# A gated recurrence and a maxout layer on one core: a shorter weight conversion, joined output sums, column quarters, and new instruction lists

## The chip, the cores and the metric

The kernel runs on one core of a Trainium2 chip. A core has five engines with queues of their own: TensorE (PE in the profile; its weight loads appear as PEld), VectorE (DVE), ScalarE (ACT), GpSimd (POOL) and SyncE (SP, which here only issues DMAs). Each engine takes its instructions in program order, and they wait for each other by semaphores. The metric is device time in microseconds (us); the profile is one execution, recorded by the hardware profiler.

## The reference

The first half is a recurrence over 768 time steps for 4 batches of 8 heads, with states of 48 x 48:

```python
mag = np.sqrt(a_re * a_re + a_im * a_im)
scale = np.minimum(mag, 0.999) / (mag + 1e-06)
a_re_n, a_im_n = (a_re * scale, a_im * scale)
for t in range(S):
    new_re = ar * S_re - ai * S_im
    new_im = ar * S_im + ai * S_re
    kv = np.einsum('bhd,bhe->bhde', k[:, :, t], v[:, :, t])
    S_re, S_im = (new_re + kv, new_im)
    y[:, :, t] = np.einsum('bhd,bhde->bhe', q[:, :, t], S_re)
```

The second half takes the 3072 rows of 384 features that come out and computes

```python
h = np.maximum(np.maximum(x @ w1, x @ w2), x @ w3)
return (h @ w_out).astype(np.float32)
```

with 768 hidden features. The weights arrive as float64; everything else is float32.

## The kernel before

The sequence is cut into 24 chunks of 128 steps. Two chunks (x and y, from two batches) make a group; there are 12 groups, six along the sequence for each pair of batches. A step is named by a word, such as `csx:3`: step `cs`, chunk x, group 3.

The steps of a group, with the engine that does them:

- Gates (`gates`): `sqr sqi add lnL expw expe lne relu Lnop abs addw lnw expL mulai mulw stt atan turn` and a few more make the logarithm of the gate's size (tile `Ln`) and its angle in turns (tile `w`) from `a_re` and `a_im`. ACT does the functions, DVE the products, and two of the sums are DMAs from POOL that add in memory.
- Angles (`angles`): `cs` sums the turns along the chunk on PE, by a product with a triangular matrix: four products for a chunk, each with 64 output columns of the array and 192 moving elements. `t`, `nf`, `af`, `sa`, `sb` take off whole turns and make cosine and sine.
- Decays (`turns`): `sums` and `F` on PE sum `Ln` over parts of the chunk; `En Ek Eq` and `f0` to `f3` are their exponentials on ACT. `mk mq uk uq kEn` scale k and q by them on DVE; `tpk tpq` transpose on PE, `Kc Qc` copy the result out of PSUM.
- Scores (`factors`, `scores`): `Q1 Q2 KB QB QG` on DVE, `A` and `B` on PE, `g0` to `g3` (DVE) and `b0 b1` (ACT) fill the masked score tile `atm`.
- State and output (`state`, `outputs`): `dk` on PE, `h0` to `h3` on DVE carry the state in tiles `g`; `y` on PE gives the chunk's output, transposed, and `x` copies it into `xhx`, the features.
- Maxout layer (`up`, `seven`): `U11 U12 U01 U02` are each nine products of 256 tokens (the first digit is the half of the hidden features, the second the weight matrix); `u..` takes the larger of the two on ACT (relu) or DVE. x @ w1 is subtracted from the other two matrices beforehand (`Wg`), and its own way to the output (w1 @ w_out) is multiplied out once (`T`, `t`, `M`, `m`), so that only two matrices are left in the loop. The projection to the output is Strassen's scheme in Winograd's form: sums `S1` to `S4` on DVE, products `P1` to `P7` (four matmuls each) and `Px Py` on PE, and output sums `r1 r6 r5 r7 r57 ox oy`; `D` stores. Group 0 is done without it (`up_one`, `project`), while the sums of weights (`J`) are made.
- Weights (`weight_load`, `weight_step`): twelve blocks of 128 x 768 numbers are loaded as float64 (`WL0` to `WL11`) and turned into float32 by integer work on their two words. Step `a` (ACT) takes the size of the high word, scaled; `b` (DVE) limits it; `c` (DVE) shifts it by three bits; `e` (DVE) fills in bits of the low word; `f` (DVE) puts the sign back and writes the block to its place.

All of this is one list of words, `SCHEDULE`, that the program runs through from front to back. The class `Bound` ties each instruction to the one ahead of it on the same engine, so the list is the order of every engine's queue, the DMA queues of SP and POOL among them. `SLOTS` names, for each PSUM tile in the order in which they are made, which of four places (two banks each) it gets; `OTHER` holds the words that run on the second engine that can do them (copies, relu and absolute values on DVE, loads and sums elsewhere).

Two things in the code matter for reading the profile. Products of few rows or columns use a part of the array, by the partitions where operands and output lie, and several run at a time. The profile gives this form with every matmul, as 128*64 for 128 rows and 64 columns. And float32 products are recorded as two matmuls each.

Every operation is recorded with the line of the helper class, L210, so groups are told apart by tile names: `up` (U), `op` (P, Px, Py, O), `ot` (the output rows), `strassen` (S1 to S4), `xhx` (features, hidden features, and in the start the tile on which the weights are converted).

Of the kernel before, what the change touches and what calls it, by code (L numbers as in the profile page):

```python
# [13 lines left out]
I32 = mybir.dt.int32  # L14
# [7 lines left out]
Lrx:0 Lix:0 sqi0:0 WL0:0 sqr0:0 xor0:0 add0:0 Wa0:0 Wb0:0 Wc0:0 We0:0 Liy:0 Wf0:0 lnL0:0 expw0:0 expe0:0 relu0:0  # L22
lne0:0 Lnop0:0 Zf:0 Lry:0 sqi1:0 xor1:0 sqr1:0 WL3:0 abs0:0 add1:0 Wa3:0 half0:0 Wb3:0 Wc3:0 lnL1:0 expe1:0 expw1:0
We3:0 lne1:0 relu1:0 Lnop1:0 Wf3:0 pw0:0 lnw0:0 expL0:0 mulai0:0 abs1:0 Lrx:1 half1:0 WL6:0 mulw0:0 Liy:1 Wa6:0
Wb6:0 sumsx:0 stt0:0 Eqx:0 Wc6:0 pw1:0 lnw1:0 expL1:0 Ekx:0 mulw1:0 WL9:0 Wa9:0 mulai1:0 We6:0 Fx:0 f1x:0 sumsy:0
Wb9:0 Eny:0 Enx:0 stt1:0 T1:0 Wf6:0 Wc9:0 f0x:0 atan0:0 turn0:0 Lqx:0 csx:0 mqx:0 WL10:0 Wa10:0 We9:0 Wf9:0 atan1:0
turn1:0 Lry:1 sqr:1 t1:0 WL11:0 Lkx:0 tx:0 nfx:0 Wa11:0 Wb10:0 csy:0 afx:0 sax:0 mkx:0 Wb11:0 Wc10:0 Lix:1 sbx:0
uqx:0 sqi:1 Lix:2 Wc11:0 Lky:0 tpqx:0 ty:0 add:1 f3x:0 f2x:0 ukx:0 Fy:0 Qcx:0 We10:0 Wf10:0 nfy:0 tpkx:0 We11:0
lnL:1 WL2:0 Q2x:0 kEnx:0 Eqy:0 expe:1 Eky:0 relu:1 xor:1 expw:1 QBx:0 Kcx:0 abs:1 T2:0 T0:0 t0:0 CL:0 KBx:0 WL1:0
Wa1:0 pw:1 Q1x:0 mky:0 Wb1:0 f0y:0 f1y:0 Wc1:0 t2:0 f2y:0 Wf11:0 lne:1 Lnop:1 Ax:0 g0x:0 Lry:2 g1x:0 We1:0 g2x:0  # L30
half:1 Lqy:0 Cdx:0 f3y:0 Liy:2 Lvx:0 mqy:0 Wa2:0 Wb2:0 lnw:1 expL:1 M0:0 mulw:1 Wc2:0 M1:0 mulai:1 dkx:0 Wf1:0
stt:1 afy:0 say:0 sby:0 Wg1:0 sqi:2 WL4:0 Wa4:0 g3x:0 sumsx:1 Lrx:2 Cdy:0 sqr:2 M2:0 We2:0 QGx:0 atan:1 Wb4:0 Wf2:0
Lvy:0 Eqx:1 Enx:1 Ekx:1 uky:0 Zg:0 tpky:0 h1x:0 m0:0 m1:0 Lkx:2 Z3:0 Wg2:0 Wc4:0 uqy:0 tpqy:0 Lqx:1 Kcy:0 Qcy:0
Bx:0 b0x:0 turn:1 b1x:0 h2x:0 mqx:1 Fx:1 f0x:1 We4:0 f1x:1 Wf4:0 f2x:1 add:2 csx:1 tx:1 yx:0 KBy:0 Q2y:0 nfx:1 xx:0
h3x:0 f3x:1 lnL:2 expe:2 Q1y:0 WL5:0 Wa5:0 Lkx:1 sumsy:1 csy:1 Eky:1 ty:1 Ay:0 kEny:0 Wb5:0 WL7:0 relu:2 mkx:1
g0y:0 Wc5:0 expw:2 U01x:0 nfy:1 abs:2 u01x:0 Lvy:1 We5:0 Eqy:1 Z2:0 g1y:0 Wa7:0 QBy:0 afy:1 Wf5:0 Eny:1 g2y:0 g3y:0
Wb7:0 Wg4:0 U11x:0 xor:2 By:0 dky:0 U02x:0 Lvx:1 b1y:0 h1y:0 b0y:0 QGy:0 yy:0 addw:2 lnw:2 expL:2 xy:0 U11y:0 Wg5:0
u02x:0 U02y:0 afx:1 half:2 u11x:0 Wc7:0 lne:2 We7:0 mulw:2 mulai:2 sbx:1 h2y:0 Z4:0 sax:1 h3y:0 stt:2 atan:2 Wf7:0
U12x:0 u12x:0 say:1 sby:1 Cdy:1 WL8:0 Cdx:1 turn:2 ukx:1 uqx:1 U01y:0 u01y:0 u11y:0 Wa8:0 U12y:0 csy:2 ty:2 u12y:0
csx:2 tpqx:1 tx:2 u02y:0 Qcx:1 nfy:2 Lnop:2 nfx:2 tpkx:1 Fy:1 kEnx:1 Wb8:0 Wc8:0 We8:0 Kcx:1 Wg7:0 Wf8:0 U21y:0  # L40
Wg8:0 KBx:1 f0y:1 u21y:0 Lky:1 Lqy:1 mky:1 afy:2 sumsx:2 dkx:1 Q1x:1 f1y:1 f2y:1 f3y:1 Enx:2 U21x:0 u21x:0 afx:2
U22y:0 u22y:0 Oy:0 Lqx:2 mqy:1 uky:1 uqy:1 tpqy:1 Ekx:2 Lix:3 Q2x:1 say:2 sby:2 sbx:2 sax:2 Eqx:2 h0x:1 h1x:1 QGx:1
h2x:1 oy:0 QBx:1 mkx:2 h3x:1 Qcy:1 Q1y:1 tpky:1 Kcy:1 Ax:1 g0x:1 Q2y:1 Liy:3 sqi:3 Fx:2 sumsy:2 g1x:1 g2x:1 U22x:0
Lrx:3 u22x:0 g3x:1 f3x:2 f2x:2 f1x:2 f0x:2 Lry:3 sqr:3 add:3 lnL:3 expe:3 Ay:1 relu:3 J3:0 g0y:1 g1y:1 mqx:2 g2y:1
Bx:1 KBy:1 kEny:1 lne:3 Ox:0 Eky:2 b1x:1 Eny:2 QBy:1 b0x:1 h0y:1 ukx:2 By:1 Eqy:2 yx:1 g3y:1 xx:1 b1y:1 Lqy:2 mqy:2
Lvx:2 ox:0 Lky:2 mky:2 b0y:1 tpkx:2 expw:3 Kcx:2 uqx:2 Lnop:3 uqy:2 tpqx:2 Qcx:2 QGy:1 dky:1 h1y:1 kEnx:2 sumsx:3
uky:2 Ekx:3 h2y:1 Eqx:3 Enx:3 yy:1 xy:1 Fy:2 f3y:2 h3y:1 dkx:2 f2y:2 abs:3 KBx:2 h0x:2 h1x:2 Q1x:2 f0y:2 f1y:2
U11:1 u11:1 tpky:2 Kcy:2 Lky:3 QBx:2 QGx:2 addw:3 Lqx:3 h2x:2 mqx:3 h3x:2 xor:3 half:3 Cdx:2 tpqy:2 Qcy:2 Q2x:2
lnw:3 kEny:2 expL:3 sumsy:3 Eqy:3 Q2y:2 Eny:3 Lkx:3 mkx:3 Fx:3 Eky:3 U01:1 Ax:2 Q1y:2 J1:0 mulw:3 mulai:3 g0x:2
g1x:2 u01:1 Cdy:2 f3x:3 f2x:3 g2x:2 g3x:2 J2:0 Bx:2 f0x:3 Dx:0 f1x:3 Dy:0 stt:3 KBy:2 h0x:3 U12:1 b0x:2 b1x:2 u12:1  # L50
S3:1 Lvy:2 yx:2 U02:1 QBy:2 Lvx:3 Lry:4 atan:3 turn:3 Liy:4 csy:3 csx:3 Lix:4 Lrx:4 sqr:4 sqi:4 add:4 lnL:4 ty:3
xx:2 By:2 u02:1 Ay:2 S1:1 nfy:3 relu:4 tx:3 expe:4 S2:1 expw:4 P5:1 P6:1 g0y:2 afy:3 say:3 sby:3 nfx:3 sbx:3 g1y:2
afx:3 sax:3 abs:4 dky:2 P1:1 Lqy:3 g2y:2 g3y:2 b1y:2 J4:0 QGy:2 P7:1 Px:1 P2:1 b0y:2 h0y:2 h1y:2 ukx:3 tpkx:3 lne:4
Lnop:4 r1:1 Liy:5 mky:3 h2y:2 h3y:2 S4:1 Kcx:3 uqx:3 yy:2 Lqx:4 kEnx:3 mqy:3 tpqx:3 Qcx:3 P3:1 r6:1 xy:2 Py:1 r5:1
r7:1 P4:1 Fy:3 uky:3 r57:1 f0y:3 f1y:3 xor:4 half:4 oy:1 ox:1 Q1x:3 addw:4 dkx:3 h1x:3 Lvy:3 f2y:3 f3y:3 h0y:3
h2x:3 sumsx:4 Ekx:4 h3x:3 lnw:4 QGx:3 expL:4 Eqx:4 Fx:4 KBx:3 U11:2 Dx:1 QBx:3 mulai:4 Q2x:3 f2x:4 Enx:4 u11:2
Cdy:3 Lkx:4 f1x:4 f0x:4 U01:2 uqy:3 f3x:4 mulw:4 stt:4 atan:4 tpky:3 Kcy:3 Ax:3 g0x:3 mqx:4 g1x:3 Bx:3 g2x:3 g3x:3
b1x:3 b0x:3 u01:2 Cdx:3 turn:4 U02:2 Lrx:5 u02:2 mkx:4 kEny:3 csy:4 csx:4 tx:4 nfx:4 ty:4 nfy:4 yx:3 xx:3 sumsy:4
KBy:3 Eqy:4 Eky:4 Lry:5 S3:2 Eny:4 sqr:5 dky:3 h1y:3 h2y:3 h3y:3 tpqy:3 Qcy:3 Q2y:3 Lix:5 sqi:5 Px:2 afy:4 add:5
lnL:5 expe:5 Dy:1 U12:2 u12:2 S1:2 Py:2 P7:2 Q1y:3 relu:5 lne:5 QBy:3 afx:4 P4:2 Ay:3 By:3 expw:5 S2:2 g0y:3 sbx:4  # L60
abs:5 g1y:3 sax:4 QGy:3 ukx:4 uqx:4 P6:2 P5:2 S4:2 g2y:3 g3y:3 P2:2 P1:2 Lqy:4 r1:2 Liy:6 mqy:4 b1y:3 P3:2 b0y:3
r6:2 r5:2 r7:2 tpkx:4 r57:2 ox:2 oy:2 kEnx:4 tpqx:4 yy:3 xy:3 Fy:4 say:4 Lky:4 sby:4 mky:4 uky:4 Lnop:5 Kcx:4 uqy:4
sumsx:5 xor:5 half:5 U11:3 KBx:4 addw:5 lnw:5 expL:5 mulw:5 Lqx:5 mulai:5 Cdx:4 h0x:4 f2y:4 stt:5 f3y:4 Ekx:5 f0y:4
Lkx:5 Dy:2 Dx:2 Qcx:4 Enx:5 Q1x:4 Cdy:4 u11:3 Eqx:5 QBx:4 mkx:5 Lry:6 QGx:4 Lvx:4 U01:3 Lix:6 atan:5 Q2x:4 u01:3
f1y:4 h0y:4 U02:3 Lrx:6 u02:3 sqr:6 dkx:4 h1x:4 sqi:6 h2x:4 h3x:4 Fx:5 f0x:5 f3x:5 add:6 f1x:5 f2x:5 Ax:4 g0x:4
Lqy:5 g1x:4 Bx:4 lnL:6 expe:6 g2x:4 g3x:4 U12:3 lne:6 b1x:4 tpky:4 turn:5 mqx:5 b0x:4 tpqy:4 Qcy:4 u12:3 Lvy:4
kEny:4 S1:3 csy:5 ty:5 csx:5 Kcy:4 dky:4 nfy:5 S3:3 sumsy:5 h1y:4 h2y:4 tx:5 nfx:5 h3y:4 afy:5 yx:4 Eky:5 Eny:5
Eqy:5 afx:5 Q2y:4 Q1y:4 sbx:5 P5:3 P1:3 P7:3 Lky:5 sax:5 Ay:4 xx:4 KBy:4 ukx:5 uqx:5 Lrx:7 tpqx:5 S2:3 expw:6
relu:6 QBy:4 Lnop:6 mky:5 tpkx:5 S4:3 Kcx:5 g0y:4 Qcx:5 P6:3 Px:3 Py:3 r1:3 By:4 P2:3 P4:3 say:5 sby:5 QGy:4 g1y:4
# [973 lines left out]
```

## Time and profile before

| what | value |
|---|---|
| time before, median of 3 runs (lowest, highest) | 557.45 us (557.34, 560.97) |
| span of the profiled execution, first to last instruction | 556.9 us |
| TensorE busy | 524.6 us |
| VectorE busy | 490.4 us |
| ScalarE busy | 370.0 us |
| loads of ScalarE's function tables | 45, of 1.283 us |
| HBM read and written | 33.03 MB and 4.72 MB |
| mean granted TensorE clock | 0.988 |

A row of the profile's groups reads: engine, operation, tiles (out<-in), sizes, count | busy time in us, mean of one in ns | idle time just before them, and what ended it. A row of a stretch gives the busy time of each engine within it, with the instruction count in brackets, then the granted clock of TensorE, the busy share of the DMA engines and what they moved. A row of the timeline gives start and duration in us, engine, operation and count. "PE lag" and other sums in the prediction are worked out in its text.

### The profile page before, as it was taken

The page shows a single profiled execution, that of the slowest core. Times are in us where ns is not written, and L with a number is a line of the kernel's source. Part 1 is how long each engine was busy: PE and PEld are TensorE (multiplying, and loading weights), DVE is VectorE, ACT ScalarE, POOL GpSimd, SP SyncE. Part 2 cuts the span into 40 slices and gives each one's busy share as a digit, 9 for nine tenths or more (in the row PEclk, how much of TensorE's full clock was granted, in tenths as well). Part 3 has the DMA queues.
Part 4 walks back from the last instruction along what each step waited for, and adds up shares of the span by engine and source line. Part 5 has one row for each costly group of instructions (what it writes and reads, how often), then busy time and mean ns, then how long its engine had stood idle before and what let it go on. Part 6 is the DMA issues. An engine that isn't in the chain of part 4 may idle for free.

```text
span 556.9 us, 22739 instructions
## 1 busy us (share of the span) xinstructions
PE 524.6 (94%) x10086; PEld 449.0 (81%) x10086; DVE 490.4 (88%) x770; ACT 370.0 (66%) x652; POOL 74.4 (13%) x117
## 2 busy tenths in 40 slices
PE   1669799989999999999999999999999999999997
PEld 0356588778888898888988888988888888998986
DVE  5999999989998899999988897999999999886524
ACT  5999989867965867787766858777646855530100
POOL 8105250002030001000120200120010020000000
PEclk9869999999999999999999999999999999999999
DMA  8977976456055164235364136542361144000000
GB/s 218 287 191 156 206 154 102 78 105 123 18 108 109 21 123 77 48 63 92 68 115 82 33 61 121 110 88 50 58 126 31 32 88 82 10 31 2 7 25 29
DMA packets 142530, 49.09 MB, mean 88 GB/s; under 512 B 130528, under 2 KB 135648, under 8 KB 142432
## 3 DMA queue, kind: packets, MB, share of 16 engines
q1 hardware_dynamic: 136272, 37.77, 31.9%
q0 software_dynamic: 6160, 9.87, 10.4%
q8 instruction: 79, 1.29, 1.0%
q14 instruction: 19, 0.16, 0.1%
HBM read 33.03 MB, written 4.72 MB: 68 GB/s over the span
## 4 chain that ended last, share of the span: by engine, by line
PE 84%; DVE 6%; DMA 4%; SPq 2%; issue 1%; ACT 1%; POOL 0%; DVEq 0%
PE up L210 34%; PE op L210 24%; PE y L210 7%; PE A L210 5%; PE tp L210 4%; PE dk L210 4%; PE sums L210 3%; PE cs L210 2%; SPq L210 2%; DMA xhx<-in_moe_w_out_dram 2%; PE F L210 2%; DVE xhx L210 1%; PE B L210 1%; DMA k<-in_k_dram 1%; DMA ar<-nf 1%
## 5 line engine op out<-in xcount | busy, mean ns | idle before, releaser
L210 PE MATMUL up<-xhx,w 128*128 128x256 f32 x792 | 177.4, 382 | 0.1
L210 PEld LDWEIGHTS up<-xhx,w 128*128 128x128 f32 x792 | 148.6, 190 | 21.5 <-PE B L210 0.3
L210 ACT ACT_TABLE_LOAD x45 | 57.7, 1283 | 1.5 <-PEq L1027 0.8
L210 ACT COPY atm<-B 32x128 f32<-32x128 f32 x96 | 24.5, 255 | 36.9 <-DVE atm L210 22.9
L210 PE MATMUL op<-wo,xhx 128*128 128x192 f32 (+1 forms) x220 | 48.5, 364 | 0.0
L210 DVE TENSOR_TENSOR Q<-Q,f 112x1024 f32<-112x1024 f32 (+1 forms) x48 | 45.4, 950 | 0.8 <-ACT Q L210 0.6
L210 ACT ACTIVATE f<-F 48x232 f32<-48x232 f32 x96 | 34.4, 359 | 13.2 <-PE F L210 5.4
L210 POOL DMA_DIRECT2D ar<-nf x40 | 34.2, 1280 | 65.3 <-DVE ar L210 54.7
L210 PE MATMUL y<-atm,vb 128*32 128x64 f32 x1152 | 39.4, 221 | 1.4 <-issue 1.1
L210 PEld LDWEIGHTS op<-wo,xhx 128*128 128x128 f32 x220 | 36.5, 190 | 4.3 <-DVE q L210 0.3
L210 POOL DMA_DIRECT2D Ln<-e x11 | 11.1, 1005 | 214.6 <-ACT e L210 53.9
L210 PE MATMUL y<-QG,g 112*32 112x64 f32 x1408 | 38.4, 219 | 0.9 <-issue 0.8
L210 PEld LDWEIGHTS y<-atm,vb 128*32 128x32 f32 x1152 | 32.5, 109 | 6.4 <-issue 3.6
L210 PEld LDWEIGHTS y<-QG,g 112*32 112x32 f32 x1408 | 34.8, 109 | 1.3 <-issue 1.0
L210 DVE TENSOR_TENSOR ot<-ot,op 128x192 f32<-128x192 f32 (+1 forms) x67 | 27.1, 413 | 9.0 <-PE op L210 4.3
L210 PE MATMUL op<-wo,strassen 128*128 128x192 f32 x176 | 33.0, 331 | 0.0
L210 PE MATMUL A<-Q,K 112*32 112x80 f32 x1536 | 31.6, 234 | 1.3 <-DVE Q L210 1.3
L210 DVE COPY_PREDICATED atm<-masko,A 128x256 f32<-128x256 uint8 x72 | 31.2, 435 | 1.6
L210 PE MATMUL op<-w,strassen 128*128 128x192 f32 x176 | 32.5, 329 | 0.0
L210 PEld LDWEIGHTS A<-Q,K 112*32 112x32 f32 x1536 | 27.2, 110 | 5.0 <-issue 1.9
L210 ACT COPY Q<-tp 112x1024 f32<-112x1024 f32 x23 | 23.3, 1013 | 10.3 <-PE tp L210 10.0
L210 ACT COPY ot<-op 128x192 f32<-128x192 f32 (+1 forms) x13 | 4.5, 342 | 38.2 <-PE op L210 38.2
(151 smaller groups left out, 1120.8 us busy)
## 6 DMA issues: line engine op xcount, KB each, us to landing
ar<-in_a_re_dram SPq DMA_DIRECT2D x24, 192.0 KB, 3.7
ai<-in_a_im_dram SPq DMA_DIRECT2D x24, 192.0 KB, 3.8
q<-in_q_dram SPq DMA_DIRECT2D x96, 48.0 KB, 2.6
k<-in_k_dram SPq DMA_DIRECT2D x96, 48.0 KB, 2.9
vb<-in_v_dram SPq DMA_DIRECT2D x96, 48.0 KB, 3.1
out_dram<-ot SPq DMA_DIRECT2D x23, 192.0 KB, 2.8
Ln<-e POOLq DMA_DIRECT2D x11, 384.0 KB, 4.7
w<-L POOLq DMA_DIRECT2D x9, 384.0 KB, 4.7
```

The lines of the kernel that those rows point to most:

```text
L210: ins = f(*a, **kw)
```

## The change

1. **Weights.** The limits come first: `b` reads the high words straight from the raw block and cuts them off on both sides, keeping the sign; `a` is now a Prelu on ACT, whose slope for negative numbers gives both the size and the sign's place in the word; `c` shifts for all blocks alike; `e` writes the finished block. Step `f` is gone. Blocks 0, 3 and 6 (w1), which are used with a minus sign, get it from the scale.
2. **Output sums.** `r5` and `r7`, two additions of 192 columns, become `r75`, one addition of 2 x 192, for which the two output tiles lie in one tile `ots`.
3. **Biases.** Three columns of constants that ACT read as a bias become numbers in the instruction.
4. **cs.** Four products of 64 columns a chunk become eight of 32 columns.
5. **Buffers.** Tiles that came from pools of two (k, q, t, nf, CS, Ln, En, K, Q, ot) get two fixed tiles each; Ek and Eq, which shared two, have two each.
6. **Lists.** `SCHEDULE`, `SLOTS` and `OTHER` are replaced as a whole. In PE's order, steps of one kind now stand together more often: 206 runs of one kind in place of 251. The start loads the first group's k and q between weight blocks. More y, K and Q copies run on DVE.

The core of the diff:

```diff
-        if step == "a":
-            activation(out=ex.bitcast(FP), in_=high.bitcast(FP), func=AF.Abs, scale=2.0 ** -112)
-        elif step == "b":
-            dve.tensor_single_scalar(out=ex.bitcast(FP), in_=ex.bitcast(FP), scalar=LAST, op=OP.min)
+        if step == "b":
+            dve.tensor_scalar(out=ex.bitcast(FP), in0=high.bitcast(FP), scalar1=LAST, scalar2=-LAST, op0=OP.min,
+                              op1=OP.max)
+        elif step == "a":
+            activation(out=ex.bitcast(FP), in_=ex.bitcast(FP), func=AF.Prelu, alpha=-2.0 ** 32,
+                       scale=-2.0 ** -112 if i in (0, 3, 6) else 2.0 ** -112)
         elif step == "c":
-            if i in (0, 3, 6):
-                dve.tensor_scalar(out=ex, in0=ex, scalar1=3, scalar2=-0x80000000, op0=OP.logical_shift_left,
-                                  op1=OP.bitwise_or)
-            else:
-                dve.tensor_single_scalar(out=ex, in_=ex, scalar=3, op=OP.logical_shift_left)
+            dve.tensor_single_scalar(out=ex, in_=ex, scalar=3, op=OP.logical_shift_left)
         elif step == "e":
-            dve.scalar_tensor_tensor(out=ex, in0=low, scalar=29, in1=ex, op0=OP.logical_shift_right, op1=OP.bitwise_or)
-        elif step == "f":
-            dve.scalar_tensor_tensor(out=dst.bitcast(I32), in0=high, scalar=-0x80000000, in1=ex,
-                                     op0=OP.bitwise_and, op1=OP.bitwise_xor)
+            dve.scalar_tensor_tensor(out=dst.bitcast(I32), in0=low, scalar=29, in1=ex, op0=OP.logical_shift_right,
+                                     op1=OP.bitwise_or)
...
-                for j in range(2):
-                    dst, m = ps[j * L64:(j + 1) * L64, ch * HC:(ch + 1) * HC], slice(ch * L64, (ch + 1) * L64)
-                    mm(out=dst, lhsT=upto[:, m], rhs=every(T["w", g][:, c * DM:(c + 1) * DM], j), start=True, stop=True)
+                for o in (0, L64, 32, L64 + 32):
+                    j, m = o // L64, slice(ch * L64 + o % L64, ch * L64 + o % L64 + 32)
+                    mm(out=ps[o:o + 32, ch * HC:(ch + 1) * HC], lhsT=upto[:, m],
+                       rhs=every(T["w", g][:, c * DM:(c + 1) * DM], j), start=True, stop=True)
...
-                activation(out=CS[:, :, 0], in_=hv(T["af", x]), func=AF.Sin, scale=TWOPI, bias=hpi)
+                activation(out=CS[:, :, 0], in_=hv(T["af", x]), func=AF.Sin, scale=TWOPI, bias=-0.5 * math.pi)
...
-                out, in0, in1 = {"r6": (yl, xl, r.get(6)), "r5": (xr, yl, r.get(5)), "r7": (yl, yl, r.get(7)),
+                if name == "r75":
+                    two_ = ot.rearrange("p c n -> p (c n)")[:, NH:3 * NH].rearrange("p (u n) -> p u n", u=2)
+                    again = yl.rearrange("p (u n) -> p u n", u=1).to_broadcast([P, 2, NH])
+                    dve.tensor_tensor(out=two_, in0=again, in1=ps[:, 1, 0:DM].rearrange("p (u n) -> p u n", u=2), op=OP.add)
+                    return
```

The lists of group 2's output, before and after (words of other groups and engines stand between them in both):

```diff
-S3:2 Px:2 S1:2 Py:2 P7:2 P4:2 S2:2 P6:2 P5:2 S4:2 P2:2 P1:2 r1:2 P3:2 r6:2 r5:2 r7:2 r57:2 ox:2 oy:2
+S3:2 S1:2 P1:2 r1:2 P5:2 S2:2 S4:2 P6:2 r6:2 Py:2 P4:2 P7:2 Px:2 r75:2 r57:2 oy:2 P2:2 P3:2 ox:2
```

## The prediction

> **What bounds the kernel now.** I read the page's busy times first, then the stretches, then TensorE's timeline.
>
> ```profile
> PE 524.6 (94%) x10086; PEld 449.0 (81%) x10086; DVE 490.4 (88%) x770; ACT 370.0 (66%) x652; POOL 74.4 (13%) x117
> ```
>
> The average points at TensorE (PE). Which engine ends the waits is a matter of the stretch:
>
> ```profile
> core 0: us, PE busy (x) PEld busy (x) DVE busy (x) ACT busy (x) POOL busy (x), PEclk, DMA share, GB/s
> 0.00:10.00 10.00, 0.00 (x0) 0.00 (x0) 3.58 (x13) 4.64 (x10) 7.57 (x33) 1.00 0.74 168
> 10.00:20.00 10.00, 7.80 (x68) 3.45 (x72) 9.63 (x18) 9.25 (x20) 6.37 (x13) 1.00 1.09 335
> 39.70:76.20 36.50, 32.57 (x672) 22.86 (x670) 36.36 (x57) 33.58 (x59) 14.14 (x18) 1.00 0.84 179
> 76.20:122.00 45.80, 43.45 (x1010) 35.39 (x1009) 43.88 (x68) 38.52 (x71) 6.33 (x7) 1.00 0.55 94
> 122.00:553.40 431.40, 430.24 (x8237) 379.62 (x8236) 376.74 (x587) 264.49 (x464) 40.01 (x48) 1.00 0.35 66
> ```
>
> From 122 us to PE's last product at 553.4, PE stands for 1.2 us in all: there only PE's own work counts. Before 76 us VectorE (DVE) is full (36.36 of 36.50) and ScalarE (ACT) nearly so; they decide when PE gets its lead of work. After PE's end 3.5 us remain (two additions and the store).
>
> What PE's work costs besides its products, the timeline shows. Columns: start, duration, tile form of the array (rows*columns), records (two to a float32 product):
>
> ```profile
> 144.74 0.49 PE L210 MATMUL cs<-w,upto 128*64 128x192 f32 x4
> 145.17 0.46 PE L210 MATMUL B<-QB,KB 112*32 112x32 f32 x32
> 145.44 1.33 PE L210 MATMUL A<-Q,K 112*32 112x80 f32 x64
> 146.71 0.59 PE L210 MATMUL op<-wo,strassen 128*128 128x192 f32 x2
> ...
> 504.69 1.14 PE L210 MATMUL dk<-vb,uk 64*64 64x48 f32 x64
> 505.76 1.31 PE L210 MATMUL A<-Q,K 112*32 112x80 f32 x64
> 507.01 4.15 PE L210 MATMUL up<-xhx,w 128*128 128x256 f32 x18
> 511.09 1.31 PE L210 MATMUL A<-Q,K 112*32 112x80 f32 x64
> 512.22 0.48 PE L210 MATMUL B<-QB,KB 112*32 112x32 f32 x32
> 512.63 0.59 PE L210 MATMUL op<-wo,xhx 128*128 128x192 f32 x2
> ```
>
> A takes 1.25 us to the next start when `up` follows (505.76 to 507.01, from 32 columns to 128), and 1.13 when B follows (511.09 to 512.22, the same form). B takes 0.41 before `op` and 0.27 before A. So **a change of tile form costs PE 0.12 us** (0.12 and 0.14 here; 0.10 for F: 0.38 before `sums`, 0.48 before A), and PE has five forms: 128 columns (up, op, wm, wt, pw), 64 (cs), 32 (A, B, y), 64*64 (sums, dk, F), 64*112 (tp).
>
> Last, the rows for the operations that are edited:
>
> ```profile
> L210 PE MATMUL cs<-w,upto 128*64 128x192 f32 x192 | 20.0, 350 | 4.8 <-DVE w L210 4.5 <-ACT Q L210 0.2
> L210 DVE TENSOR_SCALAR xhx<-xhx 128x768 f32<-128x768 f32 x12 | 7.5, 621 | 2.8 <-ACT xhx L210 2.7
> L210 DVE SCALAR_TENSOR_TENSOR w<-w,xhx 128x768 int32<-128x768 int32 x3 | 2.9, 952 | 0.0
> L210 DVE TENSOR_TENSOR ot<-ot,op 128x192 f32<-128x192 f32 x46 | 16.1, 351 | 5.9 <-ACT ot L210 3.7 <-PE op L210 1.3
> L210 ACT ACTIVATE e<-e,biases 128x768 f32<-128x768 f32 x7 | 6.6, 938 | 0.0
> L210 ACT ACTIVATE e<-e 128x768 f32<-128x768 f32 x4 | 3.4, 844 | 0.1
> ```
>
> **The change, part by part.** The profiled execution spans 556.9 us; the median of the runs is 557.45, 0.55 more for what lies around the span. I work in differences and add them to the median.
>
> 1. *New lists, PE's order.* Counting changes of form in PE's program order: 190 before; 122 after, with cs put among the 32-column kinds. With cs as a form of its own it would be 143, so the quarters are worth 21 changes and the order 47. PE's products are otherwise the same in number and size. 68 x 0.12 = **-8.2 us**, and 54 of the 68 lie behind the first full `up` of group 1 (the 122 us mark), where PE never waits. By 0.09 and 0.14 a change it is -6.1 and -9.5. I keep 0.12, read at A, PE's frequent case.
>
> 2. *cs in quarters, its own work.* Four products of 64 columns, two at a time, become eight of 32 columns, four at a time: two rounds of 192 columns either way. A pair of cs takes 1.45 us to the next start (83.92 in the chain of waits); less one change that is 0.665 a chunk. `up` takes 1.70 ns a column (3.91 us over 9 x 256); y, a 32-column kind, takes 115 ns a round of 64 columns (1.73 less 0.12, over 14 rounds), 6 ns more than its columns. So a quarter round is 0.332 and a chunk 0.664. The nearest row of eight products of 192 columns, four at a time, is `sums`: 0.67 to 0.70 (127.05 to 127.75). I take 0.66, -0.1 us for 24 chunks, by y's form; the ends are -0.3 (columns alone, 0.652) and +0.8 (`sums` at 0.70). The Trainium skill (TensorEngine Tiling (Array Packing), Instruction Overhead) speaks against it: some 60 cycles for each matmul, so 96 more would be about 2.4 us by an estimate at 2.4 GHz, and the sum 2.5 us later; `sums` with its eight shows no such addition.
>
> 3. *Weights a step shorter.* Of DVE's four steps a block (0.62, 0.62, 0.95, 0.95) the last goes: 12 x 0.95 = 11.4 us of DVE work, all in the first 75 us. The first step now reads every second word of the raw block, in a row of its own: between 0.62 (the same operation, contiguous) and 0.95 (the third step, which reads with that stride, but two sources). I take 0.62, the same operation; the other end is 12 x 0.33 = 4.0 us back. The Trainium skill (VectorE: DVE Perf Modes, Mode 2x_2P) lets one-source float32 operations in SBUF run at double rate with no condition on the inner stride, which gives the lower value; no row here shows it. ACT's step moves behind it and reads what DVE wrote; 0.90 as before.
>
> 4. *Joined r5 and r7.* 2 x 351 becomes 549 (the 384-wide addition): 0.15 x 11 = 1.7 us of DVE, behind PE, nothing on the path. r75 waits for P7 as well as P5, as r7 did; behind it on DVE stand r57 and ox, which free PSUM for PE and have waited for r7 so far too: no new wait. At the end r75 stands two products (2.6 us) ahead of the last addition, so the tail of 3.5 us stays. *Constant biases*: 938 to 844, 0.09 us for some 40 ACT instructions, 3.8 us of ACT; on the path only in the start (below). *Engine lists*: six more y copies, two more K or Q copies and four small operations pass from ACT to DVE, 8.0 us; DVE's list becomes 527.0 from 532.0 us of rows, ACT's 381.1 from 391.5. Both stay below PE.
>
> 5. *The start.* I take the lists as the order in time and add up rows in front of a word. DVE: sum x 0.92 (busy 490.4 over rows 532.0; neighbours overlap) + 6.8 us (its idle time up to 20 us). ACT: x 0.945 + 6.2. For before this DVE clock gives 43.0 for the first A (trace 42.2), 61.3 for the first y (61.2), 74.0 for the second (74.5), 121.2 for the first full `up` (122.0). PE's **lag** is that clock less PE's own work up to there: at the word U02 of group 1, 139.0 - 102.2 = 36.8. After: second y, DVE 65.2, ACT 70.2, less 39.6 = 30.6 (ACT ends last; before 33.2); U02 of group 1, 128.8 - 96.4 = 32.4; P4 of group 2, 183.5 - 151.8 = 31.7; then it falls (24 at P4 of group 3), so PE stays behind nobody. 36.8 to 32.4: **-4.4 us**. Ends: -0.7 with step 3 at its dear end (4.0 x 0.92 = 3.7 given back), and -6.2 if only ACT's 30.6 holds.
> SP's loads: k and q of the first group move between weight blocks, the second group's gates behind five of them. At the trace's 1.68 MB by 10 us and 335 GB/s after it, the latter land at 22.6 us and are wanted at 25; the first k lands at 12.6, wanted at 11.4 by DVE's clock but 15 by ACT's. Up to 2 us may go there, covered by the later maximum of the lag. POOL issues the same 65 accumulating DMAs at 13% busy: nothing. Named buffers in place of pools are as many (Ek and Eq get two each, where they shared two): no new wait.
>
> 6. *Longer runs of one form* hold more of the four PSUM tiles at once. Before, 145 changes behind 122 us cost 1.2 us of waits. Ends: 0 and 9 (0.1 us at each of 91). I take +1.
>
> Sum: -8.2 - 0.1 - 4.4 + 1 = -11.7; 557.45 - 11.7 = **545.75, say 545.7 us**.
>
> **Rivals.** (a) *The fewer changes come back as waits*: each of the 91 longer runs waits 0.1 us for a copy out of PSUM. For it: ACT's waits for tp are 10.0 us now, so copies follow their products closely. Against: PE had none behind 122. 545.7 + 8 = 553.7, within 1%. (b) *The start gives nothing*: the strided step at 0.95 and late loads hold DVE's clock where it was. 545.7 + 4.4 = 550.1. (c) *Prelu is not in the loaded table*: each of the 12 conversions brings a load and a load back, 24 x 1.283 = 30.8 us on ACT, which is full there; 11 of them lie before the second y: 70.2 + 28.2 - 39.6 = 58.8 of lag in place of 32.4, so 572.1: slower than before. It decides from about 11 loads (13.5 us: the 11.7 and ACT's 1.8 of slack). Against: the built list has 45 loads, as before, and the trace of before has just these 45. The Trainium skill (ScalarE: Activation LUTs, Table sets) counts relu, copy, identity and abs into every set, without Prelu, and has the compiler put in missing loads; by that rule (c) can happen.
>
> **How the numbers follow.** Forecast 0.68, (b) 0.13, (a) 0.12, (c) 0.04, starvation beyond (a) 0.03. A measurement of this kernel tells about 1% from no change: below 551.9 is faster, above 563.0 slower. Forecast, less 0.01 at its edge, and (b) give 0.80 faster; (a) and that edge 0.13; the rest 0.07. The range takes the forecast's terms at their good ends, -9.5, -6.2, -0.3 and 0 (541.5; 540 with the rounding of the rows), up to (a) at 554; (c) is left out.
>
> **What would show it.** Right: A to B at 1.13 and fewer A to `up`; PE idle below 3 us behind the first full `up`; cs near 0.66 a chunk; that first `up` 7 to 9 us earlier (82.3 of PE's work and a lag of 30.6 to 32.4: 113 to 115); DVE's first step near 0.62; 45 table loads. Wrong: PE waits on ACT or DVE copies between 120 and 550 us, or a changed cost of cs or of a change of form.

## The result and the profile after

The changed kernel is slower by 58 us: 615.31 us against 557.39 (medians; 613.08 to 619.29 and 556.98 to 560.97), a ratio of 1.1018 with a 95% interval of 1.095 to 1.1086. The profiled execution took 616.04 us and spans 614.3. Two of the six runs of shift48 below, 575.39 and 575.90 us, were in a slower state; its row gives the other four, but its profile is of the run of 575.90.

The page's busy times, the packets of its instruction queue, and the engines' shares of the chain that ended last:

```profile
PE 535.4 (87%) x10278; PEld 460.0 (75%) x10278; DVE 485.4 (79%) x757; ACT 356.3 (58%) x640; POOL 73.6 (12%) x117
q8 instruction: 81, 1.33, 0.9%
PE 77%; issue 7%; DVE 7%; ACT 3%; DMA 3%; SPq 2%; DVEq 0%; ACTq 0%
```

PE is busy for 10.8 us more where the prediction took 8 away, and its share of a longer span fell from 94% to 87%. "issue", time in which an engine waited for nothing that the profile shows, is 7% of the chain.

The stretches, with columns as in the prediction:

```profile
core 0: us, PE busy (x) PEld busy (x) DVE busy (x) ACT busy (x) POOL busy (x), PEclk, DMA share, GB/s
20.00:40.00 20.00, 12.59 (x196) 8.53 (x196) 18.48 (x32) 18.17 (x29) 0.00 (x0) 0.74 0.85 199
40.00:60.00 20.00, 15.46 (x70) 8.52 (x68) 17.27 (x27) 15.28 (x25) 9.12 (x9) 0.83 1.02 218
60.00:122.00 62.00, 54.38 (x1289) 45.46 (x1288) 51.90 (x84) 45.91 (x84) 9.60 (x11) 0.97 0.63 126
122.00:340.00 218.00, 195.19 (x3980) 171.58 (x3984) 184.14 (x277) 134.96 (x239) 20.06 (x24) 0.98 0.37 70
340.00:550.00 210.00, 191.77 (x3880) 170.55 (x3874) 167.28 (x262) 116.98 (x215) 20.15 (x24) 0.98 0.28 55
```

Two things differ from before. Behind 122 us, where PE stood for 1.2 us in all, it now stands for 22.8 us of the first 218 and 18.2 of the next 210. And between 20 and 60 us DVE, full before, is no longer full. PE's waits say what it stands for (us in total, times, longest):

```profile
PE y L201 <- issue: 13.9, 13, 3.1
PE F L201 <- DVE Ln L201: 10.7, 1, 10.7
PE cs L201 <- DVE w L201: 6.0, 2, 3.4
PE A L201 <- issue: 5.5, 3, 2.8
PE op L201 <- ACT ot L201: 5.2, 4, 3.9
PE op L201 <- DVE ot L201: 4.8, 6, 1.2
PE dk L201 <- issue: 4.0, 3, 1.6
```

The long waits for `Ln` and `w` belong to the start; before had such waits there too. New are the waits on "issue", in the middle of steps that need nothing any more. PE's timeline around two of them (start, duration, form, records; in brackets the idle time ahead and its cause):

```profile
380.74 2.02 PE L201 MATMUL dk<-vb,uk 64*64 64x48 f32 x128
382.69 0.67 PE L201 MATMUL A<-Q,K 112*32 112x80 f32 x25
385.78 1.43 PE L201 MATMUL A<-Q,K 112*32 112x80 f32 x36 [2.42 <-issue]
...
391.02 0.25 PE L201 MATMUL y<-QG,g 112*32 112x64 f32 x2 [1.55 <-issue]
```

One A is cut in two, and PE stands for 2.42 us in its middle, where it waits for nothing that the profile shows. From 385.78 to 391.02 PE's queue runs through 256 instructions. I numbered that queue (weight loads, matmuls and the waits between them, 20,706 in all): every stop of this kind in the trace stands at 194 + 256k, or one instruction ahead of it, 1.25 to 1.55 us after a packet of queue q8 landed. The 81 packets hold 16,384 bytes each, and 20,706 / 256 = 80.9. So **PE's instructions arrive in blocks of 256**, and at these stops the packet for the next block had started only 0.7 to 3.7 us, mostly 1 to 2, after PE entered the one ahead of it. A float32 product is four instructions (two weight loads, two matmuls), so a block is 64 products, whether these take 2.3 us (two A of 32 products, 1.13 each) or 28 (`up`, 3.91 for nine).

With these numbers PE's standing can be split into stops at block ends (within a few instructions of one) and all other, counted from PE's first product. From before to after PE's last product moved by 57.3 us (553.4 to 610.7):

| part of PE's time | before | after | difference |
|---|---|---|---|
| standing at block ends behind 60 us | 2.3 | 38.3 | +36.0 |
| other standing up to 122 us (and all up to 60) | 15.9 | 13.5 | -2.4 |
| other standing behind 122 us | 0.2 | 12.8 | +12.6 |
| PE busy | 524.6 | 535.4 | +10.8 |

The rows add up to 57.0, within 0.3 of the whole.

The third row is waits of one engine on another. An example, again PE's timeline: a product of the output waits for ACT's copy out of PSUM (`r1`), which in ACT's new order stands behind gate and angle work.

```profile
159.52 2.11 PE L201 MATMUL op<-wo,xhx 128*128 128x192 f32 x10
165.55 2.93 PE L201 MATMUL op<-w,strassen 128*128 128x192 f32 x8 [3.92 <-ACT ot L201]
```

### The profile page after: what moved, and what is told of

Read it like the earlier page. It is cut to its first block, busy times and chain, and to the rows that moved or that the text cites. A ratio compares the mean times of both kernels' runs of the same rounds, so it can differ in the third digit from the quotient of the medians.

```text
span 614.3 us, 23065 instructions
## 1 busy us (share of the span) xinstructions
PE 535.4 (87%) x10278; PEld 460.0 (75%) x10278; DVE 485.4 (79%) x757; ACT 356.3 (58%) x640; POOL 73.6 (12%) x117
## 4 chain that ended last, share of the span: by engine, by line
PE 77%; issue 7%; DVE 7%; ACT 3%; DMA 3%; SPq 2%; DVEq 0%; ACTq 0%
PE up L201 31%; PE op L201 19%; PE y L201 6%; PE A L201 4%; PE tp L201 4%; PE dk L201 3%; PE cs L201 3%; PE wm L201 2%; PE sums L201 2%; SPq L201 2%; PE F L201 1%; PE B L201 1%; DMA xhx<-in_moe_w_out_dram 1%; DMA xhx<-in_moe_w_dram 1%; DVE ot L201 1%
## 5 line engine op out<-in xcount | busy, mean ns | idle before, releaser
L201 PE MATMUL op<-wo,xhx 128*128 128x192 f32 (+1 forms) x220 | 51.4, 375 | 2.8 <-DVE ot L201 1.7
L201 PE MATMUL y<-atm,vb 128*32 128x64 f32 x1152 | 43.4, 224 | 10.1 <-issue 8.9
L201 PE MATMUL y<-QG,g 112*32 112x64 f32 x1408 | 42.0, 222 | 5.3 <-issue 5.0
L201 DVE TENSOR_TENSOR ot<-ot,op 128x384 f32<-128x384 f32 (+1 forms) x56 | 25.5, 465 | 26.6 <-PE op L201 24.4
L201 PEld LDWEIGHTS y<-atm,vb 128*32 128x32 f32 x1152 | 35.9, 111 | 13.8 <-issue 11.3
L201 DVE TENSOR_TENSOR Q<-Q,f 112x512 f32<-112x512 f32 (+1 forms) x48 | 45.1, 952 | 1.1 <-ACT Q L201 0.7
L201 POOL DMA_DIRECT2D ar<-nf x40 | 36.8, 1454 | 65.9 <-DVE ar L201 57.2
L201 PEld LDWEIGHTS op<-w,strassen 128*128 128x128 f32 x176 | 30.0, 196 | 11.2 <-ACT ot L201 6.8
L201 POOL DMA_DIRECT2D w<-L x9 | 8.4, 928 | 239.1 <-ACT L L201 78.3
L201 DVE TENSOR_TENSOR xhx<-xhx,up 128x768 f32<-128x768 f32 x22 | 20.9, 951 | 14.4 <-PE up L201 14.3
```

Of the source, the lines that this page charges most:

```text
L201: ins = f(*a, **kw)
```

## The experiments

The theory (theory 1 in the expectations): a block needs some 3.4 us to arrive and is asked for only when PE enters the one ahead of it, so PE stands wherever 64 products in a row take less. The small products (A, B, y, `dk`, F) use up a block in 1.1 us (B, four steps of 0.27) to 2.3 (A). The new order puts them side by side: behind 60 us, 31 of after's 78 blocks hold no `up`, `op` or `wm`, where before had 6 of 75. What the theory must beat: that the edits cost the time (theory 2), that the new order makes PE wait for copies out of PSUM (theory 3), or that PE's added instructions cost in proportion. All results in one table; "stops" is PE's standing at block ends from 60 to 122 us + behind 122, "other" its other standing behind 122.

| kernel | median, us (lowest, highest) | ratio to before, 95% | stops | other | first full `up` |
|---|---|---|---|---|---|
| before | 557.39 (556.98, 560.97) | | 1.4 + 0.9 | 0.2 | 121.9 |
| after | 615.31 (613.08, 619.29) | 1.095 to 1.1086 | 7.1 + 31.2 | 12.8 | 130.5 |
| shift48 | 570.61 (566.58, 571.31) | 1.0096 to 1.0203 | 2.3 + 11.5 | 0.2 | |
| shift160 | 586.71 (583.02, 591.22) | 1.0432 to 1.0575 | 4.8 + 17.6 | 0.1 | |
| shift256 | 560.99 (557.05, 563.36) | 0.9981 to 1.0052 | 3.1 + 0.0 | 0.2 | |
| new_lists | 624.59 (622.42, 626.41) | 1.1175 to 1.125 | 3.9 + 34.6 | 12.6 | 140.4 |
| edits_old_lists_no_cs | 571.3 (569.62, 573.22) | 1.0175 to 1.0276 | 4.4 + 0.9 | 3.1 | 132.9 |
| edits_old_lists | 582.83 (581.41, 587.3) | 1.0383 to 1.0525 | 5.4 + 9.8 | 2.3 | 134.9 |
| conv_only | 571.89 (566.17, 573.61) | 1.0113 to 1.0239 | 2.6 + 1.9 | 0.6 | 130.5 |
| conv_placed | 575.75 (574.14, 577.25) | 1.0305 to 1.0369 | 2.1 + 0.7 | 4.0 | 134.0 |
| after_padded | 608.02 (605.32, 609.35) | 1.0856 to 1.0945 | 6.4 + 22.4 | 12.7 | |
| after_spread | 579.37 (577.27, 583.72) | 1.029 to 1.0391 | 2.9 + 2.9 | 4.8 | 127.4 |
| before_reordered | 576.68 (574.89, 580.36) | 1.0241 to 1.034 | 1.4 + 2.2 | 4.4 | 128.4 |

**shift48, shift160, shift256: before's kernel with 12, 40 or 64 useless products of 8 columns ahead of its first step.** Nothing else changes; they only move where the blocks end, by 48, 160 and 256 of PE's instructions.

```diff
+    idle = banks("idle", 8)
+    for _ in range(40):
+        mm(out=idle[0:8, 0:8], lhsT=biases[:, 0:1].to_broadcast([P, 8]), rhs=biases[:, 0:1].to_broadcast([P, 8]), start=True, stop=True)
```

> The kernel before with 40 products of 8 columns put ahead of its first word (160 instructions of TensorE, matmuls and weight loads together, run while TensorE has nothing to do); their results are not used, nothing else is changed. Theory 1 (TensorE's instructions arrive in blocks of 256, some 3.2 to 3.6 us a block, and a block whose work is shorter than that leaves TensorE standing): the blocks are cut at other places of the same list; working out each block's work from the trace of the kernel before with all cuts moved by 160 gives 21 to 30 us of standing in place of 0.6 to 1.6, so 578 to 587 us. Theory 2 (one of the edits costs the time) and theory 3 (waits for copies out of PSUM in the new order): no edit and no new order here, 557 to 558.5.

> The same with 64 such products, 256 instructions, a whole block. Theory 1: all cuts fall between the same instructions as before, so 557 to 560 us although more is added than with 160. If the added products themselves cost the time, it is 1.6 times what 160 instructions cost. Theories 2 and 3: 557 to 559.

> The kernel before with 12 of the useless products ahead (48 instructions), between no shift and 160. Theory 1: the cuts move by 48 instructions; by the work of each block in the trace of the kernel before, with 3.2, 3.45 and 3.6 us for a block, 11, 15 and 17 us of standing, so 11 to 18 us above the kernel before. If what costs the time in shift160 grew with the number of added instructions: 48/160 of its 27.6, 8 us, and shift256 would have cost 44. If the order or the edits cost it: no change.

PE's waits in shift160, and its only one on "issue" of over 1 us in shift256:

```profile
PE y L210 <- issue: 9.6, 10, 2.3
PE pw L210 <- ACT w L210: 6.3, 1, 6.3
PE cs L210 <- DVE w L210: 4.5, 2, 3.2
PE A L210 <- issue: 3.8, 3, 1.3
PE dk L210 <- issue: 3.0, 2, 1.7
```

```profile
PE y L210 <- issue: 3.1, 1, 3.1
```

40 products cost 27.6 us (586.71 less before's 559.09 in the same runs); 64 products, more work, cost 1.9 with an interval around nothing, because a shift by a whole block leaves every block's content as it was. In shift160 the waits on "issue" of after's trace appear in before's unchanged order, and all but one are gone in shift256. That is the sharpest of the comparisons: no explanation by dependencies or by an amount of work has room in it. shift48 comes out at 570.61, 8.8 above before's 561.83 in those runs and below the 11 to 18 that were expected: a miss. The 13.8 us of stops are those of its longest run, 14 above before; what its shorter runs stood for is not shown. A cost in proportion to what was added (48/160 of shift160's 27.6, 8.3) happens to give about the same; shift256 excludes it.

So before's order was not free of the limit. Its block ends lay where they hurt least: with 3.45 us for a block and each block's own work summed up, every shift of its order between 48 and 208 instructions gives 14 to 26 us of stops, one of up to 16 about 1, and from 208 on they fall, to 2 at 240 (worked out, not run but for the shifts above).

**stream: the price alone.** PE runs 1024 products in a row of each width, quarters of the array four at a time, without any wait, at first while 28 MB are loaded.

```python
products(ps["n%d" % c], 64 * 16, c)     # for c in 32, 64, 128, 192, 256
mixed(ps["small"], ps["big"], 16)       # seven of 32 columns, then one of the whole array with 384
```

> The rate of TensorE's instructions by itself; nothing of the reference is computed, zeros are stored. Six times 16 blocks of 256 instructions (64 products each) with 32 output columns, four at a time as in y: 64 moving columns while 28 MB are loaded, then 32, 64, 128, 192 and 256 moving columns without loads; at the end 16 blocks in which every eighth product is one of 128x384. Theory 1: a block takes the longer of its work and the time of a fetch: 3.2 to 3.6 us for 32 and 64 columns alike (their work is 1.0 and 1.8 by B and y), 3.7 for 128, 5.5 for 192, 7.3 for 256, 6 for the mixture, and 3.5 to 5 us for the loaded one. If TensorE is not bound by blocks: 1.0, 1.8, 3.7, 5.5, 7.3.

PE's timeline among the products of 32 columns, and the packets of the page:

```profile
104.16 1.93 PE L65 MATMUL n<-zeros,left 128*32 128x32 f32 x128 [1.52 <-issue]
107.62 1.93 PE L65 MATMUL n<-zeros,left 128*32 128x32 f32 x128 [1.52 <-issue]
111.07 1.93 PE L65 MATMUL n<-zeros,left 128*32 128x32 f32 x128 [1.52 <-issue]
114.80 1.93 PE L65 MATMUL n<-zeros,left 128*32 128x32 f32 x128 [1.80 <-issue]
```

```profile
q8 instruction: 112, 1.84, 1.2%
```

Each row is one block, 128 records; the next starts 3.45 us later (3.73 in some), of which PE stands for 1.52. The 64-column section keeps the same 3.45, of which PE stands for 1.46; at 128 columns a block takes its own work, 3.49 us, at 192 columns 5.20, and at 256 columns 6.91. The 28,672 instructions of PE are 112 blocks of 256, the page's 112 packets. While 28 MB are loaded (and 4.7 MB stored) a block takes 5.1 to 8.4 us, mostly 6.2, where 3.5 to 5 were expected: this traffic makes it dearer. The mixture took 8.78 us a block where 6 were expected; it has 16 changes of form a block, and at the 0.17 us that forms gives below these are 2.7 us, which would be the difference. The granted clock was 0.50 in the steady part of the 32-column section and 1.00 in the 64-column one, and the block takes 3.45 us in both.

The Trainium skill (Runtime: NRT & Kernel Launch, Instruction fetch mechanics) describes such blocks, 16 KiB or 256 instructions, the next one fetched while the current one runs. The trace agrees: packets of 16,384 bytes, stops 256 apart, one block ahead. The Trainium skill also calls the crossing mostly hidden; here the runs differ from it, with 3.45 us a block and 38.3 us of standing in this kernel, and the measurement decides.

**new_lists, edits_old_lists and edits_old_lists_no_cs: lists or edits?** new_lists is after with its lists and fixed buffers and constant biases, but the old conversion, r5 and r7 apart and cs in halves. edits_old_lists is after's code on before's lists, and the third is the same with cs in halves. In these two, and in conv_placed below, one load of k into a fixed buffer (`Lkx:2`) stands ahead of the steps that still use the group before (`mkx:1`, `ukx:1`): they do the same work, but on the next group's k. Their DVE also waits 1.7 to 3.6 us for a load of q, which before and conv_only do not.

```diff
-                for o in (0, L64, 32, L64 + 32):
+                for j in range(2):
...
-Wb0:0 ... Wa0:0 ... Wc0:0 ... We0:0
+Wa0:0 ... Wb0:0 ... Wc0:0 ... We0:0 ... Wf0:0
...
-r75:2
+r5:2 r7:2
```

> The lists of the kernel after with the edits undone: old weight conversion (a and b exchanged back, f put behind e), cs in halves, r5 and r7 apart. The fixed buffers and the constant biases stay. Theory 1 (blocks of 256 instructions of TensorE that the new order fills with small products): taking the 384 instructions of the quarters out of the trace of the kernel after leaves 30 to 37 us of standing, so 608 to 625 us. Theory 2 (an edit costs the time): 555 to 570. Theory 3 (the new order makes TensorE wait for copies out of PSUM): 600 to 620 too, but with the copies as what ends the waits.

> The kernel after, but with the lists of the kernel before (step f struck out, a and b exchanged, r75 in the place of r7) and with cs in halves as before. TensorE has the instructions of the kernel before in the same order, so its blocks are cut alike. Theory 1: 546 to 555 us, below the kernel before by what the shorter conversion gives at the start (0 to 11 us). Theory 2, with the conversion, r75, biases or buffers as the culprit: above 590. Theory 3: 546 to 555.

> The same with cs in quarters: all edits of the kernel after, on the old lists. Each cs now has 16 instructions more, 384 in all. Theory 1: the cuts drift through the list; worked out on the trace of the kernel before with 16 instructions put in at each cs, 15 to 23 us of standing, less some 2.5 for 21 changes of tile form that go: 11 to 20 us above the run without the quarters. Theory 2 with cs as the culprit: 50 us above it. Theory 3, and the prediction's own steps: 2 to 3 us below it.

The lists alone give 624.59, more than the whole change: the 38 us of stops and the 13 us of other waits come with them. The edits on before's lists cost some 12 us without cs and 23.7 with it. The 11.5 between them is mostly what the cs quarters do to the blocks: 16 more instructions a chunk, 384 in all, that move every block end behind them (stops 5.3 without, 15.2 with). Their own work is what the prediction said (below). That the edits without cs cost 12 us and do not gain was expected by nobody; conv_only takes it up.

**after_padded and after_spread: mend the blocks, keep the rest.** after_padded adds 113 useless products at ten places of after's order, chosen by the block sums. after_spread keeps after's edits and its number of instructions; PE's and DVE's steps behind 60 us move by a few places, so that a large product lands in most blocks.

```diff
+PADS = {'sumsy:0': 26, 'yx:0': 24, 'csx:2': 3, 'tpqx:3': 4, 'yx:3': 4, 'Ay:7': 15, 'csy:9': 2, 'Fx:9': 8, 'Fx:10': 21, 'Ay:9': 6}
...
+        for _ in range(PADS.get(T.get("word"), 0)):
+            mm(out=ps[0:8, 0, 0:8], lhsT=biases[:, 0:1].to_broadcast([P, 8]), rhs=biases[:, 0:1].to_broadcast([P, 8]),
```

> The kernel after with 113 useless products of 8 columns (452 instructions, 0.066 us a product or 7.5 us in all) put in at ten places of TensorE's list, so that the cuts between blocks fall where less time is lost: worked out on the trace of the kernel after, the standing falls from 37 to 21.5 us. Theory 1: 605 to 610 us, faster with more work. Theory 3, or if the products are simply added work: 620 to 625.

> The kernel after with the same words, edits and DMA and ScalarE orders, but TensorE's and VectorE's words behind 60 us moved by a few places each, so that a large product (up, P) comes into most blocks of 256 instructions; the places of the PSUM tiles follow. By the durations of the traces, and 3.45 us as the least time of a block (measured in the stream of products), the standing at the cuts falls from 46 us to 6 in the list alone; changes of tile form rise somewhat. Theory 1: standing at the cuts under 10 us in the trace and 555 to 575 us in all, 40 to 60 below the kernel after with not one instruction of the kernel fewer. If the cuts are not what costs the time (theory 3: waits for copies in an order like this one): 595 to 615.

The padded kernel does more work and is faster by 7 us, with 9.5 us fewer stops (15.5 were expected). after_spread is 36 us faster than after, though 4 above the 575 of its forecast; its busy line and PE's longest waits on "issue":

```profile
PE 534.4 (93%) x10278; PEld 451.1 (78%) x10278; DVE 481.0 (83%) x757; ACT 355.8 (62%) x640; POOL 74.3 (13%) x117
PE y L202 <- issue: 3.1, 5, 1.0
PE dk L202 <- issue: 2.0, 1, 2.0
```

The stops fell by 32.5 us, from 38.3 to 5.8, with PE's products unchanged in number, and the other waits by 8.0; 4 of 77 blocks are left without a large product. But it has 201 changes of form, more than before's 190: what fills the blocks is the very alternation that the new lists had removed. No list here has both the saving of the prediction's first term and full blocks; that none can is not shown.

**before_reordered: can before be mended the same way?** Before's code, its PE and DVE steps moved likewise.

> The kernel before, no edit, with TensorE's and VectorE's words behind 60 us moved by a few places in the same way, blocks kept as well filled as they are. Theory 1: standing at the cuts stays under 4 us, so within 549 to 560 us; whether it beats the kernel before depends on 9 us of waits and changes of form that were traded, so this tells only whether a list can be redone at all if the cuts are counted.

A miss: it is 15 us slower than before, although its stops are small. It has 214 changes of form, and its first full `up` comes 6.5 us later, with 4.4 us of waits behind it. No version here beats the kernel before.

**conv_only and conv_placed: the shorter conversion alone.** conv_only is before with the new steps b, a, c, e in place of a, b, c, e, f, in the old places. conv_placed has all the edits but cs, with b and a both at a's old place and e at f's.

> The kernel before with the shorter weight conversion alone (steps a and b exchanged in the list, e at the place of f, pools of buffers kept). TensorE's list is untouched, so theory 1 expects under 3 us of standing at cuts. The prediction's own step: 11.4 us less of VectorE's work before the first full up, so 550 to 556. If the earlier runs of the edits on the old lists lost their 12 to 19 us because ScalarE's step now stands behind VectorE's in lists made for the other order: 565 to 575; if the fixed buffers cost it: 550 to 557.

> All edits but the quarters of cs on the old lists, as in edits_old_lists_no_cs, but with b and a both at the old place of a and e at the old place of f. There ScalarE waited 10.9 us for b in the first 75 us, since a stood in front of the other functions while b stood late in VectorE's queue. If the place of the steps cost the 12 us of that run: 549 to 557 us, with the first full up before 122 us. If the shorter conversion itself costs the time: 565 or more. TensorE's instructions are those of the kernel before, so theory 1 expects under 3 us of standing.

conv_only's stretches in the start:

```profile
20.00:40.00 20.00, 9.83 (x111) 7.11 (x104) 16.32 (x27) 18.93 (x32) 0.00 (x0) 0.58 0.80 200
40.00:60.00 20.00, 17.01 (x184) 10.20 (x183) 15.62 (x25) 17.63 (x28) 7.74 (x13) 0.93 0.66 126
```

The same stretches of before:

```profile
20.00:40.00 20.00, 10.83 (x112) 7.62 (x104) 19.93 (x31) 19.80 (x33) 0.00 (x0) 0.66 0.88 220
40.00:60.00 20.00, 19.35 (x283) 12.19 (x282) 19.93 (x30) 18.92 (x28) 10.40 (x13) 1.00 0.79 169
```

A wait of ACT in conv_only:

```profile
ACT xhx L205 <- DVE xhx L205: 7.6, 5, 2.3
```

DVE's work is 10 us less (480.1 against 490.4 us), as foreseen. But DVE is not full any more: 31.9 us of work in these 40, where before had 39.9. In the old conversion ACT's step came first and could run ahead of DVE. Now DVE's b comes first, ACT waits for it (7.6 us), and DVE for ACT in turn. The first full `up` comes at 130.5, 8.6 later than before, with nearly the same stops. conv_placed, with b earlier, made ACT wait 16.5 us for DVE's step and missed too: 575.75, where 549 to 557 were expected if the place of the steps was the cause. So moving b did not mend it, and which of these waits costs the time stays open.

**forms: the price of a change of form by itself.** Products of 192 columns, so that the supply doesn't bind; two kinds take turns in 4, 16 and 64 pieces of the same total.

```python
whole(w, 64 // pieces)
quarter(o, 256 // pieces, P) if other == "quarter" else half(o, 128 // pieces)
```

> Nothing of the reference is computed; zeros are stored. Products of 192 columns in nine stretches: products of the whole array (128*128) and quarter products (128*32, four at a time) take turns in 4, 16 and 64 pieces, so 8, 32 and 128 changes of tile form with the same products; then whole and half products (64*64, two at a time) likewise; then quarter products of 128 rows and of 112 rows, which the prediction counted as one form. A block of 256 instructions holds at least 5.2 us of work everywhere, so the supply does not bind. By the prediction's price of 0.12 us a change, the stretch of 64 pieces is 14.4 us longer than that of 4 (120 changes) with quarters and with halves, and the two are equal within 1 us with rows. If the price read at A belongs to A alone (its short runs, its copies), 64 and 4 pieces differ by less than 4 us: then the saving of the prediction's first term was never there. If a change of rows alone costs the same, the stretches with rows differ by 14 us, and the prediction counted too few changes in both orders.

PE's timeline at 16 and at 64 pieces:

```profile
90.05 1.51 PE L60 MATMUL other<-zeros,left 128*32 128x192 f32 x32
91.48 1.57 PE L65 MATMUL whole<-zeros,left 128*128 128x192 f32 x8
...
136.03 0.53 PE L60 MATMUL other<-zeros,left 128*32 128x192 f32 x8
136.50 0.59 PE L65 MATMUL whole<-zeros,left 128*128 128x192 f32 x2
```

Whole and quarter products took 42.83, 46.96 and 63.04 us in 4, 16 and 64 pieces, whole and halves 42.88, 47.12 and 63.68: 0.17 us a change in both (20.2 / 120, 20.8 / 120). So the price is real, and here dearer than the prediction's 0.12. Quarters of 128 and of 112 rows took 20.84 and 20.87 us in 4 and 16 pieces, so a change of rows costs nothing, as assumed. (Their third stretch, 41.91, shows only that pieces of two products use half of the four places.)

## Why the prediction was wrong, point by point

- **Longer runs of one form (term 6: +1, ends 0 and 9): the step that failed.** It asked what longer runs do to PSUM and put a copy's wait on each. What they did is to fill blocks of instructions with small products: +36.0 us of stops, shown by shift160 against shift256, and by after_spread. The other waits behind 122 us, +12.6, are mostly the kind that rival (a) named (PE for a copy or sum of an `op` tile, 10.0 us over the whole trace), but few and long, up to 3.92, and above its 8. The waits of before, 1.2 us in all, could not bound this: that order hid the supply, and the page's packets of q8 (79, 1.0% of the DMA time) entered no term.
- **Changes of form (term 1: -8.2).** The count and the price hold: 190 and 122 changes, two A together take 2.23 us to the next start (513.49 to 515.72 in after's timeline), 1.115 each, and forms has 0.17. The sum isn't seen: PE's busy time went up by 10.8. By tiles, y grew by 4.3 us, `op` by 3.4, `wm` by 2.6, A by 1.4, cs by 1.3, B by 1.0; others changed by less. Most of it goes with the granted clock. It was 0.50 in seven stretches of after's trace, in which PE was busy for 31.0 us, and in one of before's, with 8.5. That one, and three of after's:

```profile
24.70:38.40 13.70, 8.49 (x91) 6.52 (x92) 13.63 (x21) 13.57 (x23) 0.00 (x0) 0.50 0.84 203
```

```profile
44.40:51.20 6.80, 5.86 (x9) 3.20 (x10) 6.73 (x12) 4.98 (x10) 2.83 (x5) 0.50 1.09 222
163.80:170.60 6.80, 5.05 (x14) 4.44 (x15) 4.71 (x8) 5.67 (x10) 1.49 (x3) 0.50 0.14 25
385.70:389.10 3.40, 3.32 (x116) 3.32 (x120) 1.61 (x3) 0.00 (x0) 0.05 (x1) 0.50 1.02 187
```

  The stretch at 44.40 lies in `wm`; in that at 163.80, eight records of `op` take 2.73 us to the next start (165.55 to 168.28), where eight of that size take 1.50 in forms, at a clock of 1.00. If work takes twice as long there, the stretches make (31.0 - 8.5) / 2 = 11.3 us, an estimate, and that is all of the 10.8. Each of the six behind 40 us begins in a stop of PE of 1.6 to 3.9 us or within 0.6 us of its end, but stops of that length stand elsewhere without one, so what makes the clock fall stays open. So does where the 8.2 us went: by the same estimate after's busy time at the full clock would be within 1 us of before's. Stops that the busy time does not show as idle may be part of it: after_spread, with 79 changes more (9.5 us at 0.12), is busy for 1.0 us less than after, and the clock (0.50 for 18.5 us of its busy time) makes up some 6 of these 10.5.
- **cs in quarters (term 2: -0.1).** Right for its own work: 0.67 us a chunk to the next start on the average, its changes of form included, and 0.655 between two A (1.31 a pair, no change), where before had 0.73. The rows of the trace of after for this and the next terms:

```profile
L201 PE MATMUL cs<-w,upto 128*32 128x192 f32 x384 | 21.4, 345 | 8.8 <-DVE w L201 6.0 <-issue 2.8
L201 DVE TENSOR_TENSOR ot<-ot,op 128x384 f32<-128x384 f32 x32 | 17.3, 550 | 10.3 <-PE op L201 10.1
L201 ACT ACTIVATE xhx<-xhx 128x768 f32<-128x768 f32 x12 | 10.1, 841 | 1.6 <-DVE xhx L201 1.6
L201 DVE TENSOR_SCALAR xhx<-xhx 128x768 f32<-128x768 f32 x4 | 2.2, 558 | 1.9 <-DMA xhx<-in_moe_w_dram 1.4 <-DMA xhx<-in_moe_w_out_dram 0.5
```

  The Trainium skill's overhead of some 60 cycles a matmul (TensorEngine Tiling (Array Packing), Instruction Overhead) would have added 2.4 us by the prediction's estimate; the trace shows no such addition. What the term missed is that 384 instructions move the block ends: +11.5 us on before's lists, 9.9 of them stops.
- **The weights (term 3).** DVE's work fell as worked out, and the strided first step costs 0.558 us (the fourth row; 0.55 to 0.60 in eleven blocks, 1.65 in the first), no more than a contiguous one. The Trainium skill (VectorE: DVE Perf Modes, Mode 2x_2P) gives one-source float32 operations in SBUF the double rate and names no condition on the inner stride; the trace agrees, with the 0.558 us.
- **Joined sums, biases (term 4).** r75 takes 0.550 us (second row, 0.549 forecast), the Prelu 0.841 (third row). Whether r75 stood on the path was not told apart from PE's other waits for DVE's `ot`, 4.8 us.
- **The start (term 5: -4.4, first full `up` at 113 to 115).** Wrong in sign: 130.5. The step that failed is the clock made of sums: "DVE: sum x 0.92" holds while DVE is full. With less to do DVE was not full but waited: conv_only has 10 us less of DVE work and the same 130.5. On PE, "other standing" up to 122 us fell by 2.4, but 7.1 us of stops stand between 60 and 122. How much of the 130.5 belongs to the conversion's order and how much to the new lists isn't told apart, as both alone give that much or more (130.5 and 140.4).
- **Rivals.** (c) is out: 45 table loads of 1.283 us, as before. (b) gave 550.1 and (a) 553.7. The waits of (a) came, dearer than it had them. Of (b)'s two causes the strided step at 0.95 did not come; DVE waited 5.4 us in all for weight blocks; and the start lost 8.6 us where (b) had nothing gained. The range, 540 to 554, held only what rows of before's trace showed as waits, and starvation beyond (a) had 0.03.

## What to carry to other kernels

Before reordering products on PE, sum up each block of 256 instructions (64 float32 products) and compare it with 3.45 us: products of equal form bunched together may save 0.12 to 0.17 us a change and lose up to 3 us a block. A change of PE's instruction count anywhere moves all block ends behind it, so two versions that differ by a few small products can differ by 5% without any of their steps being worse; shift by a whole block to test for it. And a clock made of an engine's summed work holds only while that engine is full: shorten its work, or put another engine between its steps, and the waits must be summed anew.

## What was not expected of the hardware

PE's instructions come at no more than a block of 256 in 3.45 us (stream), 5.1 to 8.4 us under loads, one block ahead: the profile shows it only as "issue". A change of tile form costs 0.17 us of PE between products of 192 columns, and a change of rows alone nothing (forms). The granted clock was 0.50 where PE was kept waiting for 1.52 of every 3.45 us, at 32 columns, but 1.00 right behind it, at 64 columns, with 1.46 of 3.45: such waiting alone does not settle it. In after it was 0.50 for 3.4 or 6.8 us at a time, beginning in or right behind stops of 1.6 to 3.9 us, at a price of some 11 us by the estimate above.
